# Loading weight tiles early, converting the first two sooner, moving the first up product and scaling chunk 3 sooner: one change to the start of a fused retention and MLP kernel

## The chip, the cores and the metric

The kernel runs on one core of a Trainium2 chip. The metric is device time in microseconds (us). Engines are called as in the profile: PE is TensorE (PEld its weight loads), DVE is VectorE, ACT is ScalarE, POOL is GpSimd, SP the queue that issues the loads.

## The reference, cut to what matters

```python
# retention: B=4, H=8, S=768, D=64, float32
for t in range(S):
    state = gamma * state + k[:, :, t] (outer) v[:, :, t]
    y[:, :, t] = scale * q[:, :, t] @ state
x = y.transpose(0, 2, 1, 3).reshape(3072, 512)
# MLP: w_in 512 x 2048, w_out 2048 x 512
h = x @ w_in
g = h - tanh(h)
out = g @ w_out
```

The two weight matrices arrive in double precision. q, k and v are float32.

## The kernel before

The retention is done in 24 chunks of 128 tokens. A chunk is scaled, k and q are transposed on PE, products give the masked scores and the state, and `outputs` and `outputs_rest` give y, which ScalarE copies to xT. The MLP then takes 256 tokens at a time: an up product `h`, a chain of activations called shrink on ScalarE and VectorE, and a down product `o`. The two are interleaved in one hand-written order. In these traces each engine does its instructions in the order of the program, so an instruction's place in the list of its engine matters as much as its data: raw tile 4 left the load queue at 23.6 us, and ScalarE, busy with other activations, first read it at 43.73.

The weights' 32 raw tiles are converted to float32 on the chip. Each conversion is two steps on ScalarE, four on VectorE, two on GpSimd:

```python
nc.scalar.activation(head.bitcast(F32), hi.bitcast(F32), AF.Abs)
nc.scalar.activation(low, lo, AF.Copy, scale=2.0 ** -52)
nc.vector.tensor_scalar(head..., HI_MIN, HI_MAX, op0=ALU.max, op1=ALU.min)
nc.vector.tensor_scalar(head, head, 3, 0x3FFFFFF8, ...)
nc.vector.scalar_tensor_tensor(head, in0=hi, scalar=0xC0000000, in1=head, ...)
nc.vector.tensor_scalar(power, head, 0xFF800000, None, op0=ALU.bitwise_and)
nc.gpsimd.tensor_tensor(low, low, power.bitcast(F32), op=ALU.mult)
nc.gpsimd.tensor_tensor(dst, low, head, op=ALU.add)
```

Tiles 0 and 1 are what the first up product multiplies by, tiles 2 and 3 the second; tiles 4 and 5 belong to the first down product. The start of the order, which the change touches:

```python
load_chunk(0); load_chunk(1); load_weights(0); load_weights(1); load_chunk(2)
# ... chunks 0 and 1 scaled, transposed; products(0)
outputs(0); products(1); outputs_rest(0)
load_chunk(3); load_weights(2); convert(0); load_weights(3)
outputs(1); convert(1); load_weights(4); outputs_rest(1)
scale_chunk(2, nc.vector); turn(2, "o"); turn_copy(2)
up_step(0)
products(2)
scale_chunk(3, nc.vector); turn(3, "o"); turn_copy(3)
convert(2); load_weights(5); outputs(2); products(3); outputs_rest(2)
load_chunk(4); convert(3); outputs(3); load_chunk(5); load_weights(6)
outputs_rest(3)
shrink_step(0); up_step(1); convert(4); load_weights(7)
shrink_step(1); scale_chunk(4); convert(5); load_weights(8)
up_step(2); turn(4); turn_copy(4); shrink_step(2)
downs(LAG)        # the first down product
# ... (cut)
```

(Statements are joined on lines here.) A raw tile has three buffers, so tile i can be loaded only when tile i-3 has been read (in the trace of this kernel the load queue waited 67.0 and 88.2 us in total for VectorE to have read a raw tile).

## Time and profile before

| | before |
|---|---|
| median, three runs first taken | 791.33 us |
| PE busy, whole span | 759.3 us of 789.4 (96%) |
| PE idle before 85 us | 25.3 us |
| PE waits of that, longest | 5.3 us for tile 5, 4.5 us for the first load of k, 2.8 us with nothing visible that held it ("issue"; called fetch stall below, as it ends at 18.22, 2.7 us after a packet of the page's queue "q8 instruction" begins at 15.54), 1.7 us each for VectorE's scaled q of chunk 2, for that of chunk 3, and for tile 3 |
| PE's mean granted clock, 20 to 60 us | 0.76 |

What is to be won lies in the first tenth of the run, where PE alternates between short attention work and waits. The prediction shows the lines and reads them.

### The profile page before, as it was taken

What the parts mean: (1) busy time and instruction counts of PE and PEld (TensorE: products, weight loads), DVE (VectorE), ACT (ScalarE), POOL (GpSimd) and SP (SyncE); (2) the same over time, 40 slices, a digit from 0 to 9 for tenths busy, and PEclk for the clock granted to TensorE, in tenths of its full rate; (3) what the DMA queues carried; (4) which work ended last, traced back from release to release, by engine and by line L of the source; (5) the groups of instructions that cost most, each with busy time, mean ns of one, the idle gap of its engine ahead of it and who ended that gap; (6) DMA issues with size and microseconds to landing.
All of it is one profiled execution on the core that took longest, in us unless ns stands there. A gap on an engine that the chain in (4) does not pass through costs nothing.

```text
span 789.4 us, 13758 instructions
## 1 busy us (share of the span) xinstructions
PE 759.3 (96%) x5504; PEld 511.7 (65%) x5504; DVE 522.1 (66%) x806; ACT 370.5 (47%) x661; POOL 126.5 (16%) x108
## 2 busy tenths in 40 slices
PE   4769999999999999999999999999999999999997
PEld 3545666667667767666666666666666666666664
DVE  3586598788888865576665565666565666655654
ACT  3363565666565554444444443344444434444432
POOL 1354454433445341000000000000000000000000
PEclk9777999999999999999999999999999999999999
DMA  9465564453343422000000000000000000000000
GB/s 209 123 158 122 122 149 107 119 132 100 95 116 99 94 55 69 29 37 18 1 27 1 0 27 0 1 27 1 1 26 1 27 1 0 27 0 1 27 0 27
DMA packets 85711, 42.97 MB, mean 54 GB/s; under 512 B 76304, under 2 KB 76432, under 8 KB 85648
## 3 DMA queue, kind: packets, MB, share of 16 engines
q1 hardware_dynamic: 85504, 41.95, 21.1%
q8 instruction: 43, 0.70, 0.4%
q10 hardware_dynamic: 144, 0.15, 0.1%
q14 instruction: 20, 0.16, 0.1%
HBM read 35.80 MB, written 6.29 MB: 53 GB/s over the span
## 4 chain that ended last, share of the span: by engine, by line
PE 90%; DVE 6%; issue 1%; POOL 1%; DMA 1%; ACT 1%; SPq 1%; DVEq 0%; ACTq 0%; POOLq 0%
PE h L346 42%; PE o L378 41%; PE y L290 3%; PE kqTp L216 2%; PE s L250 1%; PE s L244 1%; DVE head L169 1%; DVE head L167 1%; DVE a L254 1%; DMA v<-in_v_dram 1%; SPq L192 1%; DVE power L171 0%; DVE g L370 0%; DVE head L165 0%; DVE state L267 0%
## 5 line engine op out<-in xcount | busy, mean ns | idle before, releaser
L378 PE MATMUL o<-w,g 128*128 128x512 f32 x768 | 351.8, 601 | 5.8 <-POOL w L176 5.3
L346 PE MATMUL h<-xT,w 128*128 128x256 f32 x1536 | 354.0, 384 | 1.7 <-POOL w L176 1.7
L346 PEld LDWEIGHTS h<-xT,w 128*128 128x128 f32 x1536 | 292.1, 192 | 70.7 <-issue 30.4
L378 PEld LDWEIGHTS o<-w,g 128*128 128x128 f32 x768 | 145.4, 192 | 152.6 <-issue 138.1
L355 ACT ACTIVATE u<-h 128x512 f32<-128x512 f32 x96 | 57.4, 598 | 267.6 <-PE h L346 267.6
L360 DVE TENSOR_TENSOR th<-h,th 128x512 f32<-128x512 f32 x96 | 66.2, 690 | 158.3 <-ACT th L356 158.2
L370 DVE COPY_PREDICATED g<-large,th 128x512 f32<-128x512 int32 x96 | 74.6, 777 | 9.9
L365 DVE SCALAR_TENSOR_TENSOR h<-q,h 128x512 f32<-128x512 f32 x96 | 66.8, 696 | 11.1 <-DVE h L363 1.4
L363 DVE SCALAR_TENSOR_TENSOR h<-q,h 128x512 f32<-128x512 f32 x96 | 66.9, 696 | 10.4 <-DVE h L361 0.5
L357 ACT ACTIVATE q<-u,tab 128x512 f32<-128x512 f32 x96 | 69.5, 724 | 0.0
L358 ACT ACTIVATE q<-u,tab 128x512 f32<-128x512 f32 x96 | 69.2, 720 | 0.0
L359 ACT ACTIVATE large<-u,tab 128x512 f32<-128x512 f32 x96 | 68.9, 717 | 0.0
L369 DVE TENSOR_TENSOR g<-h,u 128x512 f32<-128x512 f32 x96 | 66.3, 691 | 3.3
L361 DVE SCALAR_TENSOR_TENSOR h<-u,h 128x512 f32<-128x512 f32 x96 | 65.8, 685 | 0.0
L172 POOL TENSOR_TENSOR low<-low,power 128x512 f32<-128x512 f32 x32 | 41.2, 1288 | 151.2 <-DVE power L171 135.2
L356 ACT ACTIVATE th<-h 128x512 f32<-128x512 f32 x96 | 57.0, 594 | 0.0
L226 ACT COPY kqT<-kqTp 128x1024 f32<-128x1024 f32 (+1 forms) x28 | 24.8, 891 | 55.6 <-PE kqTp L216 55.6
L254 DVE TENSOR_TENSOR a<-s,tab 128x512 f32<-128x512 f32 x24 | 16.6, 690 | 43.8 <-PE s L250 43.8
L176 POOL TENSOR_TENSOR w<-low,head 128x512 f32<-128x512 f32 x32 | 41.4, 1293 | 2.5
L324 ACT COPY xT<-y 128x512 f32<-128x512 f32 x24 | 14.1, 587 | 53.3 <-PE y L290 53.3
L169 DVE SCALAR_TENSOR_TENSOR head<-raw,head 128x512 uint32<-128x512 uint32 x32 | 25.5, 797 | 1.1
L201 POOL TENSOR_TENSOR q<-q,tab 128x512 f32<-128x512 f32 x20 | 21.8, 1089 | 22.2 <-DMA q<-in_q_dram 22.2
(32 smaller groups left out, 360.3 us busy)
## 6 DMA issues: line engine op xcount, KB each, us to landing
raw<-in_moe_w_out_dram SPq DMA_DIRECT2D x16, 512.0 KB, 3.7
k<-in_k_dram SPq DMA_DIRECT2D x24, 256.0 KB, 4.6
q<-in_q_dram SPq DMA_DIRECT2D x24, 256.0 KB, 5.1
v<-in_v_dram SPq DMA_DIRECT2D x24, 256.0 KB, 5.4
out_dram<-sum SPq DMA_DIRECT2D x24, 256.0 KB, 2.0
raw<-in_moe_w_in_dram SPq DMA_DIRECT2D x16, 256.0 KB, 3.0
raw<-in_moe_w_in_dram SPq DMA_DIRECT2D x32, 128.0 KB, 3.5
tab<-in_tables_dram ACTq DMA_DIRECT2D x1, 145.5 KB, 2.5
```

The source lines that it names most:

```text
L346: nc.tensor.matmul(hp[:, ts(i, TH)], w1[:, c, ts(2 * m2 + i, P)], xT[n // 2][:, c, ts(n % 2, TH)], start=(i == 0 and c == 0), stop=(c == N ...
L355: nc.scalar.activation(u, hp, AF.Square)
L357: nc.scalar.activation(q0, u, AF.Square, bias=bias0)
L358: nc.scalar.activation(q1, u, AF.Square, bias=bias1, scale=math.sqrt(A))
L359: nc.scalar.activation(large, u, AF.Relu, bias=bias_m)
L360: nc.vector.tensor_tensor(th, hp, th, op=ALU.subtract)
L361: nc.vector.scalar_tensor_tensor(hp, in0=u, scalar=R, in1=hp, op0=ALU.subtract, op1=ALU.mult, reverse0=True)
L363: nc.vector.scalar_tensor_tensor(hp, in0=q0, scalar=C0, in1=hp, op0=ALU.add, op1=ALU.mult)
L365: nc.vector.scalar_tensor_tensor(hp, in0=q1, scalar=A * C1, in1=hp, op0=ALU.add, op1=ALU.mult)
L369: nc.vector.tensor_tensor(flat, hp, u, op=ALU.mult)
L370: nc.vector.copy_predicated(flat, large.bitcast(I32), th)
L378: nc.tensor.matmul(o_p[j], gT[n, m2][:, i, ts(j, P)], w2[:, 2 * m2 + i], start=(first and i == 0), stop=(last and i == 1))
```

## The change

It means to have the first weights converted earlier, and to keep the load queue from waiting for raw buffers. The chunk buffers of x (tag xT) are five, and three of them are not needed until later, so six raw tiles (3 to 8) are put there. Chunk loads and weight loads move forward accordingly. Tile 0 is converted ahead of chunk 0's output, tile 1 ahead of chunk 1's, and tile 1's last two steps go to VectorE. The first up product stands ahead of chunk 2's transposes, and chunk 3 is scaled before chunk 2's products.

```diff
+            if 3 <= i < 9:
+                if i % 2:
+                    room[0] = xp.tile([P, 2, 2 * BANK], U32, tag="xT", name=f"raws_{i}")
+                raw = room[0][:, (i + 1) % 2]
+            else:
+                raw = stage.tile([P, 2 * BANK], U32, tag="raw", name=f"raw_{i}", bufs=3)
...
-    def convert(i):
+    def convert(i, engine=nc.gpsimd):
...
+    convert(0)
     outputs(0)
     products(1)
     outputs_rest(0)
     load_chunk(3)
-    load_weights(2)
-    convert(0)
-    load_weights(3)
+    for i in range(2, 6):
+        load_weights(i)
+    convert(1, nc.vector)
     outputs(1)
-    convert(1)
-    load_weights(4)
     outputs_rest(1)
+    load_chunk(4)
+    load_weights(6)
+    load_weights(7)
+    up_step(0)
     scale_chunk(2, nc.vector)
     turn(2, "o")
     turn_copy(2)
-    up_step(0)
+    scale_chunk(3, nc.vector)
     products(2)
-    scale_chunk(3, nc.vector)
     turn(3, "o")
     turn_copy(3)
     convert(2)
...            (the later loads move forward in the same way)
```

More of the change, by code (lines that the diff above doesn't have):

```diff
@@ L108 @@
     raws = {}
+    room = [None]
     NW = 2 * NM
@@ L131, in load_weights @@
         if w_out.dtype != F32:
-            raw = stage.tile([P, 2 * BANK], U32, tag="raw", name=f"raw_{i}", bufs=3)
+            if 3 <= i < 9:
[4 more added lines that the diff above has]
+                raw = stage.tile([P, 2 * BANK], U32, tag="raw", name=f"raw_{i}", bufs=3)
             raws[i] = raw
@@ L171, in convert @@
         nc.vector.tensor_scalar(power, head, 0xFF800000, None, op0=ALU.bitwise_and)
-        nc.gpsimd.tensor_tensor(low, low, power.bitcast(F32), op=ALU.mult)
+        engine.tensor_tensor(low, low, power.bitcast(F32), op=ALU.mult)
         head = head.bitcast(F32)
@@ L175, in convert @@
             low, head = (t.rearrange("p (k n) -> p k n", k=2) for t in (low, head))
-        nc.gpsimd.tensor_tensor(dst, low, head, op=ALU.add)
+        engine.tensor_tensor(dst, low, head, op=ALU.add)
     loaded = {}
@@ L458 @@
     convert(2)
-    load_weights(5)
     outputs(2)
@@ L462 @@
     outputs_rest(2)
-    load_chunk(4)
+    load_chunk(5)
     convert(3)
     outputs(3)
-    load_chunk(5)
-    load_weights(6)
     outputs_rest(3)
+    load_weights(8)
+    load_chunk(6)
     shrink_step(0)
@@ L471 @@
     convert(4)
-    load_weights(7)
     shrink_step(1)
@@ L475 @@
     convert(5)
-    load_weights(8)
     up_step(2)
@@ L484 @@
     convert(6)
-    load_chunk(6)
     load_weights(9)
```

## The prediction

> **What bounds the kernel now.** I first read the page's busy line by slices: TensorE (PE) is 90% or more in every slice from the eighth on, and low only in the first five (about 99 us); its granted clock is below full only there.
>
> ```profile
> span 789.4 us, 13758 instructions
> PE   4769999999999999999999999999999999999997
> DVE  3586598788888865576665565666565666655654
> PEclk9777999999999999999999999999999999999999
> DMA  9465564453343422000000000000000000000000
> ```
>
> Then busy time by stretches (columns: stretch, length, busy us of PE, PE weight loads, VectorE, ScalarE, GpSimd, each with its count, then PE clock, DMA share, GB/s):
>
> ```profile
> 0.00:20.00 20.00, 9.51 (x256) 7.92 (x256) 7.51 (x14) 6.40 (x13) 2.60 (x6) 0.93 1.09 209
> 20.00:60.00 40.00, 27.48 (x340) 20.87 (x336) 28.30 (x47) 20.51 (x39) 16.44 (x14) 0.76 0.51 142
> 60.00:85.00 25.00, 22.67 (x374) 14.24 (x372) 14.05 (x23) 8.96 (x18) 12.05 (x12) 0.83 0.57 131
> 85.00:130.00 45.00, 44.45 (x640) 32.39 (x641) 38.79 (x60) 28.86 (x53) 20.77 (x17) 1.00 0.57 131
> 130.00:337.00 207.00, 207.00 (x2354) 141.71 (x2353) 160.05 (x265) 115.40 (x212) 74.64 (x62) 1.00 0.35 89
> ```
>
> From 85 us PE is full, and the change leaves PE's list the same length. So the time can only move by PE's idle time before 85 us: 10.49 + 12.52 + 2.33 = 25.3 us, plus what the reduced clock costs there. The rest will only shift.
>
> Third, the chain that ended last, between 14 and 60 us (start, length, what):
>
> ```profile
> 14.74 0.69 PE y L290 x30
> 15.42 2.79 issue
> 18.22 0.83 PE y L290 x14
> ...
> 22.34 0.61 DVE q L201
> 22.95 0.04 issue
> 23.00 1.12 PE kqTp L216 x4
> 24.12 5.30 PE h L346 x16
> 29.42 0.62 PE s L244 x32
> ...
> 32.06 0.61 DVE q L201
> 32.67 0.14 issue
> 32.81 0.64 PE kqTp L216 x4
> ...
> 42.75 1.28 POOL w L176
> 44.03 0.04 issue
> 44.08 4.73 PE h L346 x12
> ...
> 57.92 1.28 POOL w L176
> 59.20 0.04 issue
> 59.24 5.49 PE o L378 x6
> ```
>
> PE is held four times: 2.8 us for nothing visible at 15.4, by VectorE's scaling of chunk 2 (23.00) and of chunk 3 (32.81), by weight tile 3's conversion (44.08), by tile 5's (59.24). The list of waits agrees: matmul h waits 1.7 us and matmul o 5.3 us for GpSimd's last conversion step.
>
> Did any conversion wait for its load? Raw tile 4 left the queue at 23.6 us and 3.4 to 5.3 us is what these tiles take to land, but ScalarE first read it at 43.73, behind five activations. Tile 5 left at about 36.3 and was read at 51.63; tile 7 at about 48.0 and 67.89. No load is late. What is late is each conversion's place in ScalarE's and VectorE's lists.
>
> [...] the clock is 0.50 in 20 to 25 us, and the last 12 matmuls of a 16-matmul product took 4.73 us at 44.08 where a whole one takes 3.45 later. [...] the shift step (line 167) takes 0.43 us, but 1.37 when begun at 38.62 during GpSimd's add (38.32 to 39.71). [...] The trace shows 43 such packets, 0.70 MB[...]: PE stops after about 444 matmul and weight-load instructions and again (0.66 us at 36.6) after about 952, 508 apart[...]. The packets began at 15.5 and 34.3 us.
>
> **The change part by part.**
>
> (a) First up product. Before, chunk 1's output ends on PE at 20.22, but its copy to xT queues behind tile 1's two activations on ScalarE and ends at 21.34; PE does chunk 2's transposes, waits, and starts the product at 24.12. After, tile 1's activations lie before that output, the copy runs at once (0.59 us), and the transposes come later: start at 20.22 + 0.04 + 0.59, about 21.0. Is tile 1 ready? VectorE now converts tile 0 (2.1 us) before chunk 1's mask and states, ending near 17; it then does four steps for tile 1 (2.1 us) and both last steps in GpSimd's place, 2 x 0.69 = 1.4 instead of 2 x 1.29. Even if GpSimd's work on tile 0 blocks it to about 18.0 it ends near 21.5, and the product first needs tile 1 after a quarter of its matmuls. Gain here 3.1 us. The 5.3 us length I leave at about 5.2, mostly at half clock; end 26.2.
>
> (b) The moved transposes. Chunk 2's two groups now stand behind the product: 1.1 us, and products of chunk 2 wait for the second copy (0.59), so their end is 26.2 + 1.1 + 0.1 + 0.6 + 0.75 = 28.75, against 30.50 before: 1.75 left of the 3.1.
>
> (c) Chunk 3 scaled earlier. Before, VectorE scaled it after chunk 2's mask and states; its transposes ended 2.94 us after chunk 2's products. After, that scaling is long done and they take 1.25: 30.0 instead of 33.44. Gain so far 3.4 us.
>
> (d) Tiles 2 and 3. Their order on ScalarE and VectorE after chunk 3's transposes is unchanged. Before, tile 2's VectorE part started at 34.67 and tile 3 was finished at 44.02, 9.35 us later[...]. After, 31.25 + 9.35 = 40.6. Gain 3.4.
>
> (e) Instruction fetch. [...] The early loads make DMA busy there: about 2.35 MB more (tile 5, chunk 4, tiles 6 and 7) at the 0.22 MB/us of the first 28 us fills 28 to 38 us. [...] So the stall may grow from 0.66 to 1.5 or 3 us; chunk 2's last copy and tile 3's activations lie behind it, with some 0.9 us to spare against VectorE's chain. I take off 0.4.
>
> (f) Early raw loads. They remove waits of the DMA queue (raw tiles waited 67 and 88 us in total for VectorE to free a buffer), none of which PE sees. Chunk 7's scaling waited 2.45 us for its load at 80.7, but PE had other work. Zero.
>
> (g) Behind tile 3: second product, its shrink, tile 5, first down product keep order and length. Tile 5 ends near 55.8 instead of 59.2. All that follows shifts.
>
> Sum: 3.1 - 1.35 + 1.65 - 0.4 = 3.0 us[...]. 791.3 - 3.3 = 788.0.
>
> **The rivals.** First, the wait merely changes its name: tile 3's conversion holds the second product whenever the first is done, because convert(2) and convert(3) keep their places. For it: both are released by ScalarE's list, and VectorE's two steps are on the chain from 34.67 to 41.3. Against: that list itself hangs on chunk 3's transposes, which do come sooner. It would leave 0 to 1 us, 790.5 to 791.3. Second, fetch and DMA: under heavier traffic PE's instructions or chunk 3 come 2 to 3 us later. For it: the 2.79 us stall under full load; against: these fetches are few. Result 790 to 791.5, with bad luck 792. Third, loads were the limit after all, and the 5.3 us wait at 59.24 goes too: 783. Against: the 20 us between tile 4's issue and its first use. Fourth, the clock: [...] That is plus or minus 1.5 us.
>
> **Range and chances.** The sum is 3.3 us[...], and one side open by a shorter wait for tile 5: 785.0 to 790.8 should hold it 8 times in 10. Faster by over 2% would need 15.8 us, most of the 25.3 us of early holes: 2 in 100. Slower by 2% would need a new wait in each of the later steps, which the unchanged order forbids: 1 in 100. Within 2%: 97 in 100.
>
> **What would show it.** Right: the first 16-matmul h group starts near 21 and ends near 26; chunk 3's transposes come without a wait for VectorE; the second h product still waits for GpSimd's conversion, ending near 40.6; the first o group still waits 4 to 6 us and resumes near 56; from 85 us on the same rows about 3 us earlier. Wrong: an issue stall over 2 us between 30 and 36; the wait for tile 3 or tile 5 gone; the h group starting after 23; or later stretches with PE under 99%.

The sum came to 3.3 us: 3.0 us from the steps (a) to (e), and 0.3 us for the clock. The clock's term was the author's estimate, not shown by a trace. "Such packets" are those of "q8 instruction". That PE waits for them is the reading of their times: in the kernel before, the stalls end 2.7 and 2.3 us after packets that begin at 15.54 and 34.3.

## The result, and the profile after

Six runs each, taken together: 788.44 us median (786.5 to 789.02) against 791.63 us (789.71 to 793.42) for the kernel before. The ratio is 0.9957, interval 0.9939 to 0.9976: 0.4% faster, inside the 2% that count as the same. Ratios here are the mean time of one kernel's fast runs over that of the other's fast runs of the same rounds, so not quite the ratio of the medians.

The stretches of the changed kernel (columns as in the prediction):

```profile
0.00:20.00 20.00, 9.85 (x240) 7.94 (x240) 10.00 (x18) 6.80 (x12) 2.81 (x6) 0.96 1.09 204
20.00:60.00 40.00, 29.32 (x350) 21.89 (x351) 27.72 (x47) 19.96 (x39) 14.70 (x12) 0.76 0.72 186
60.00:85.00 25.00, 22.26 (x410) 15.26 (x409) 13.76 (x23) 10.97 (x22) 11.69 (x10) 0.88 0.47 105
85.00:130.00 45.00, 45.00 (x610) 31.71 (x609) 39.12 (x62) 29.19 (x54) 21.75 (x18) 1.00 0.50 117
```

VectorE does 10.0 us of work in the first 20 us instead of 7.5, because the conversions have moved there. PE's idle time in 20 to 60 us falls from 12.5 to 10.7 us; over the whole span PE is busy 759.3 and 758.9 us, so most of the gain is idle time. From 85 to 130 us PE is now full, where the kernel before still had 0.55 us of holes. The spans, 789.4 and 786.7 us, differ by 2.7 us, which is already there at 57 us. The chain that ended last shows it (start, length, what):

```profile
16.88 0.46 PE y L297 x14
17.34 1.76 issue
19.10 0.83 PE y L297 x14
...
21.17 0.59 ACT xT L331
21.76 0.14 issue
21.90 5.26 PE h L353 x16
27.16 0.45 PE kqTp L223 x4
...
39.75 1.28 POOL w L183
41.03 0.04 issue
41.07 5.08 PE h L353 x12
...
55.29 1.27 POOL w L183
56.56 0.04 issue
56.61 5.49 PE o L385 x6
```

Against the kernel before, the first h product begins at 21.90 instead of 24.12, tile 3's conversion ends at 41.03 instead of 44.03, and tile 5's at 56.56 instead of 59.20. The two waits behind those conversions remain: PE's idle time for tile 5 is 5.3 us in both, that for tile 3 is 2.24 us instead of 1.70. In this profile the change moves the whole stair, that is, the row of waits one behind the other, by 3.0 us at tile 3 and 2.6 us at tile 5. The two waits of 1.7 us for VectorE's scaled q of chunks 2 and 3 are gone; the fetch stalls and the waits for the two conversions stay.

### The profile page after: what moved, and what is told of

The parts are those of the page before. It is cut to its first block, busy times and chain, and to the rows that moved or that the text cites. A ratio compares the mean times of both kernels' runs of the same rounds, so it can differ in the third digit from the quotient of the medians.

```text
span 786.7 us, 13754 instructions
## 1 busy us (share of the span) xinstructions
PE 758.9 (96%) x5504; PEld 511.9 (65%) x5504; DVE 522.2 (66%) x808; ACT 370.2 (47%) x661; POOL 123.7 (16%) x106
## 4 chain that ended last, share of the span: by engine, by line
PE 92%; DVE 4%; SPq 1%; issue 1%; ACT 1%; POOL 1%; DMA 1%; DVEq 0%; POOLq 0%; ACTq 0%
PE o L385 42%; PE h L353 42%; PE y L297 3%; PE kqTp L223 2%; PE s L257 1%; PE s L251 1%; SPq L199 1%; DVE head L176 1%; DVE head L174 1%; DMA raw<-in_moe_w_in_dram 1%; DVE a L261 0%; DVE power L178 0%; POOL low L179 0%; POOL w L183 0%; DVE head L172 0%
## 5 line engine op out<-in xcount | busy, mean ns | idle before, releaser
L179 POOL TENSOR_TENSOR low<-low,power 128x512 f32<-128x512 f32 x31 | 39.6, 1277 | 157.4 <-DVE power L178 153.7
L183 POOL TENSOR_TENSOR w<-low,head 128x512 f32<-128x512 f32 x31 | 39.8, 1283 | 2.4
L297 PEld LDWEIGHTS y<-kqT,state 64*64 64x64 f32 x704 | 12.9, 134 | 17.9 <-issue 11.7
```

## The experiments

Twelve kernels ran in three batches, each with the kernel before beside it (medians 791.62, 791.78 and 791.64 us). Five runs undo one part of the change each, two keep one part or two, four go further, one repeats the change. The change has a sixth part that no run undoes alone: tile 1's place ahead of chunk 1's output. The changed kernel itself ran only in the first batch and in the rounds of the result, so comparisons with it from the other two batches go across batches; the third batch ran on another chip (recorded as 4, the others as 2), where the kernel before had nearly the same median.

First a warning that these runs taught. Run after run of one kernel differs by up to 5 us (788.9 to 793.9 for the kernel before), largely in step with the granted clock. Of the 31 runs of the kernel before in the three batches, 17 had a mean clock of 0.980 and a median of 792.2 us; the 14 with 0.984 to 0.989 had 789.7 us. The changed kernel (12 runs) shows the same: nine at 0.982 with a median of 788.5 us, three at 0.984 to 0.987 with 786.5 us. Each kernel has one trace (the changed kernel two, both of the low class), so the cause is read across kernels. There the difference is a lower granted clock late in the start. It meets, or does not meet, the same eight matmuls of the second down product, as in the changed kernel (first line, run at 0.982; clock 0.68 over these matmuls, 0.50 from 74 to 76 us) and in one of the experiments (up0_back, second line, run at 0.987; clock 1.00 from 70 to 76 us):

```profile
72.62 5.40 PE L385 MATMUL o<-w,g 128*128 128x512 f32 x8
```

```profile
71.52 4.05 PE L385 MATMUL o<-w,g 128*128 128x512 f32 x8
```

That is 1.35 us with no change to what these instructions wait for. The six matmuls behind the wait for tile 5 give another 0.95 us (5.49 and 4.54 us, at a mean clock of 0.50 and 0.63). Where it matters below, medians are also compared at like clock: the low class up to 0.983, the high class from 0.984. This comparison is rough. The high class of the changed kernel has three runs, the class reaches from 0.984 to 0.991, single runs fall outside the pattern (793.9 us at 0.987), and the mean clock may itself be partly an outcome of the change: the nine runs of tile5_earlier and late_tile5, in which most of PE's 5.3 us wait for tile 5 is gone, were all at 0.984 to 0.986. But so were the five runs of tile1_pool, at 0.984 to 0.987, in which that wait stays.

### after_again: the changed kernel once more

No edit.

> The changed kernel once more, as the yardstick of this batch: about 0.9957 of the kernel before, 788.4 us, with the first h product beginning near 21.9 us, the second held until about 41.0 and the first o group until about 56.6.

788.33 us, ratio 0.9967 (0.9945 to 0.9988). The repeat holds in time, but its profiled execution (789.97 us, the slowest of its six) has a different shape: the first product began at 21.44, and the second fetch stall was long. Here is the same instruction in the first profile and in this one; the bracket is PE's idle time before it, "issue" meaning that nothing visible held it:

```profile
33.45 0.33 PE L297 MATMUL y<-a,v 64*64 64x64 f32 x4 [0.42 <-issue]
```

```profile
35.98 0.33 PE L297 MATMUL y<-a,v 64*64 64x64 f32 x4 [2.48 <-issue]
```

Tile 3 was then waited for until 42.5 and tile 5 until 58.2, against the expected 41.0 and 56.6. So the growth of this stall that the prediction's step (e) feared exists, but not in every execution. Against the kernel before, this profile has only 1.6 us of the gain at tile 3 and 1.1 us at tile 5.

### late_loads: the change without its loads

```diff
-            if 3 <= i < 9:
-                ...                      # room of the x buffers
-            else:
-                raw = stage.tile(..., bufs=3)
+            raw = stage.tile(..., bufs=3)
# and every load_weights and load_chunk back where the kernel before has it
```

> The changed order of conversions, scalings and products, but every raw tile in its three old buffers and loaded where the kernel before loads it. My theory (the loads were never late, the order is what gains): the same as the changed kernel within 0.5 us, about 788.4, PE's waits for tiles 3 and 5 ending near 41 and 56.5. The rival (the early loads gain): back to about 791.5.

787.76 us, ratio 0.996 (0.9941 to 0.9978). No loss at all; at low clock 788.0 against the changed kernel's 788.5. PE waits for tile 3 until 40.44 and for tile 5 until 55.92. The second fetch stall is absent: the waits of PE list one "issue" wait before y, of 1.6 us, instead of two. The waits for tiles 3 and 5 are there as in the changed kernel:

```profile
40.44 8.47 PE L347 MATMUL h<-xT,w 128*128 128x256 f32 x28 [2.19 <-POOL w L177]
55.92 5.49 PE L379 MATMUL o<-w,g 128*128 128x512 f32 x6 [5.27 <-POOL w L177]
```

The rival, that the early loads gain, falls.

### loads_only: the kernel before with the early loads alone

```diff
# the changed kernel, with the compute order of the kernel before:
-    convert(0)
     outputs(0)
...
+    convert(0)
     outputs(1)
+    convert(1)
# and the up product and chunk 3's scaling in their old places
```

> The kernel before with the early loads alone, its order of work untouched. My theory: about 791.6, no gain, tile 3's wait ending near 44 and tile 5's near 59 as before; PE's fetch stalls may grow by some tenths under the heavier traffic. The rival: about 788.4.

792.24 us, ratio 1.002 (0.9998 to 1.0041). The early loads gain nothing here either, and may cost some tenths. Two waits of PE in its trace are longer than in the kernel before (1.74 us for q of chunk 2, 0.66 us of "issue" there):

```profile
24.00 1.11 PE L223 MATMUL kqTp<-tab,q 128*128 128x128 f32 x4 [3.01 <-DVE q L208]
39.48 0.33 PE L297 MATMUL y<-a,v 64*64 64x64 f32 x4 [1.75 <-issue]
```

Tile 3 is waited for until 46.21 and tile 5 until 61.67, not near 44 and 59 as expected. That is one profiled execution; the interval of the times reaches 1. What is shown is that no gain comes from the loads; whether they cost something stays open.

### up0_back: the first up product back behind chunk 2's transposes

```diff
-    up_step(0)
     scale_chunk(2, nc.vector)
     turn(2, "o")
     turn_copy(2)
+    up_step(0)
     scale_chunk(3, nc.vector)
     products(2)
```

> The changed kernel with the first up product back behind chunk 2's transposes and copy. By the changed kernel's times the transposes would end near 23.2, the product near 28.4, and chunk 2's products, whose copies are then long done, near 29.6, where the changed kernel has 29.5. So my theory: no difference within 0.5 us; what counted was that VectorE and ScalarE were ready, not which of the two PE did first. The rival (that order is the gain): 2 to 3 us more.

786.31 us, ratio 0.994 (0.9919 to 0.996): not slower, and by the medians 2 us faster than the changed kernel. At like (high) clock it is 786.3 against 786.5 us, no difference. Five of its six runs are of the high class, three of twelve for the changed kernel. Whether the order itself makes the good clock more frequent, or chance did, these runs can't settle. The trace agrees with the expectation:

```profile
21.87 1.12 PE L223 MATMUL kqTp<-tab,q 128*128 128x128 f32 x4 [0.65 <-DVE q L208]
22.78 5.26 PE L353 MATMUL h<-xT,w 128*128 128x256 f32 x16
```

The transposes still come first, but wait 0.65 us for VectorE's scaled q instead of 1.74, because VectorE has tile 1 behind it earlier. The product begins at 22.78, 1.1 us sooner than in the kernel before (23.91 by the same view), and chunk 2's products need no wait for the copies behind it. Tile 3's wait ends at 40.76, where the changed kernel has 41.07.

### scale3_back: chunk 3's scaling back behind chunk 2's products

```diff
-    scale_chunk(3, nc.vector)
     products(2)
+    scale_chunk(3, nc.vector)
     turn(3, "o")
```

> The changed kernel with chunk 3's scaling back behind chunk 2's products on VectorE. My theory: chunk 3's second transposes wait some 1.5 us for VectorE again and everything behind them moves, 1.5 to 2 us more than the changed kernel, about 790.2. The rival (that wait was hidden behind another): no difference, 788.4.

788.95 us, ratio 0.9976 (0.995 to 1.0002). The old wait is back, at its old length of 1.71 us (the changed kernel has none there):

```profile
31.47 0.85 PE L223 MATMUL kqTp<-tab,q 128*128 128x128 f32 x4 [1.71 <-DVE q L208]
```

Tile 3 is waited for until 43.24 and tile 5 until 59.18, 2.2 and 2.6 us later than in the changed kernel's first profile, but only 0.7 and 1.0 us later than in its second (after_again). The median moves by only 0.6 us, less than expected, with five of its six runs in the high clock class. There it is 788.4 against 786.5 us, 1.9 us more, as expected. The classes are small (five and three runs), so the size is rough; the returned wait is plain.

### tile0_later: tile 0 converted behind chunk 0's output

```diff
-    convert(0)
     outputs(0)
     products(1)
     outputs_rest(0)
+    convert(0)
```

> The changed kernel with tile 0's conversion back behind chunk 0's output. My theory: converting tile 0 first is what made the first h product begin at 21.4 to 21.9 instead of the predicted 21.0, since chunk 1's mask and state now stand behind four VectorE steps; so y of chunk 1 no longer waits for VectorE's state near 16, the h product begins near 21.0, and the time is 0.5 to 1 us less than the changed kernel's. The rival (the fetch stall at 15 to 19 us sets that start whatever VectorE does): no difference.

789.19 us, ratio 0.9965 (0.9944 to 0.9985), and my theory was wrong. VectorE's state is no longer waited for, yet PE stands at the same place for longer, and the product begins at 21.94 as before:

```profile
19.45 0.21 PE L297 MATMUL y<-kqT,state 64*64 64x64 f32 x1 [3.58 <-issue]
21.94 1.62 PE L353 MATMUL h<-xT,w 128*128 128x256 f32 x3 [0.80 <-ACT xT L331]
```

When PE gets there earlier, the stall is longer (3.58 us against 1.76) and ends no sooner (19.45 against 19.10). The fetch stall, not VectorE, sets this start; the rival holds. The time is not better than the changed kernel's: 0.8 us more by the medians, and at high clock 789.5 (five runs) against 786.5 us. Its trace has tiles 3 and 5 waited for until 42.45 and 58.25, close to after_again's 42.50 and 58.16. Whether tile 0's early place gains, these runs don't settle.

### tile1_pool: tile 1's last two steps back on GpSimd

```diff
-    convert(1, nc.vector)
+    convert(1)
```

> The changed kernel with tile 1's last two steps back on GpSimd. My theory: GpSimd would finish tile 1 near 23.1 us, and the first h product (beginning near 21.9, at half clock, its first quarter without tile 1) reaches it near 23.6, so no difference, within 0.5 us of the changed kernel. The rival (VectorE's conversion is what lets the product begin early): 1 to 1.5 us more.

786.69 us, ratio 0.9945 (0.9931 to 0.9959); all five runs of the high clock class, where the changed kernel has 786.5. No difference, as expected: GpSimd finishes tile 1 at 23.15, and the product is at work from 21.05, on its first quarter until then; its fifth matmul begins at 23.20, about 0.3 us late. Taking these steps to VectorE gained nothing that the times show.

### two_parts: only tiles 0 and 1 sooner, and chunk 3 scaled sooner

```diff
# late_loads, and in it:
-    up_step(0)
     scale_chunk(2, nc.vector)
     turn(2, "o")
     turn_copy(2)
+    up_step(0)
     scale_chunk(3, nc.vector)
```

> Only what my theory still counts: tiles 0 and 1 converted sooner and chunk 3 scaled sooner; late loads and the first up product back behind chunk 2's transposes. My theory: all of the gain and a little more, since PE has no second long fetch stall: 785.5 to 787.5, as the run with that product back (786.3). The rival (the loads and the product's place, each without effect alone, cover for each other): 790 or more.

785.81 us, ratio 0.9928 (0.9916 to 0.9941), in the expected range. So the loads and the product's place do not cover for each other: without both, the kernel is at least as fast as with both. At high clock it is 785.8 against 786.5 us; the changed kernel's 788.4 contains mostly runs of low clock. Its trace has the first fetch stall (1.7 us) and not the second.

### tile5_earlier and late_tile5: the wait that the change left

The change leaves PE's longest wait, 5.3 us for tile 5, untouched. Tile 5's conversion stands behind the second shrink on ScalarE and VectorE:

```diff
     up_step(1)
+    scale_chunk(4)
     convert(4)
+    convert(5)
     shrink_step(1)
-    scale_chunk(4)
-    convert(5)
```

> The changed kernel with tile 5's conversion right behind tile 4's, ahead of the shrink of the second product, and chunk 4's scaling ahead of both. My theory (tile 5 is late only by its place in the lists of ScalarE and VectorE, which are idle for some 4 us before that shrink): the 5.3 us wait of the first o group goes, with it the half clock behind it (its last six matmuls in 2.6 us instead of 5.5), so 6 to 8 us less than the changed kernel, about 781.5. The rival (something else holds that group next, a load, the shrink or the scaling of chunk 4): 1 to 3 us less, about 786.

783.75 us, ratio 0.9912 (0.9892 to 0.9932): 4.6 us less than the changed kernel in the same batch, below the expected 6 to 8 and above the rival's 1 to 3. But all five runs are of the high clock class; against the changed kernel's three such runs it is 2.75 us, inside the rival's range. Most of the wait went, and with it the half clock behind it (granted clock 1.00 from 54 to 58 us, where these matmuls had 0.50 in the changed kernel):

```profile
54.10 2.84 PE L385 MATMUL o<-w,g 128*128 128x512 f32 x6 [1.01 <-POOL w L183]
68.34 0.70 PE L297 MATMUL y<-kqT,state 64*64 64x64 f32 x16 [2.62 <-DVE state L270]
```

The first line is the group that began at 56.61 and took 5.49 us. The second shows where part of it was given back: VectorE, now without a hole, has the conversions of tiles 6 and 7 ahead of chunk 5's state, and PE waits 2.62 us for that instead of 0.86. The trace adds up: 4.28 us of the wait and 2.65 us of the six matmuls gained, 1.34 us lost because tile 3's wait ended later (42.41, behind a fetch stall of 2.12 us), 1.76 us lost at that state. That leaves 3.8 us, and the y group behind the second down product begins at 79.11 instead of 82.92. The rival was right that something else holds PE next, but only in part of the size.

> The kernel with the late loads (old three buffers) and tile 5's conversion ahead of the second shrink. My theory: early loads are not needed for it either, and without them the second fetch stall of PE (2.1 us near 34 in the run with the early loads) is short or gone: 1 to 2.5 us less than that run, 781 to 782.5. The rival (tile 5's earlier conversion lives on the early load): ScalarE waits for raw tile 5, 784 to 786.

783.46 us, ratio 0.9897 (0.9875 to 0.9919), with the three old raw buffers. The early load isn't needed for this either. It is hardly faster than the run with the early loads, 783.5 against 783.75 us, so the expected 1 to 2.5 us did not come. Against late_loads, of another batch, with the same buffers, it is 4.3 us less. The second fetch stall is gone, as expected, but PE waits for tile 3 until 41.52 in its profile and again 2.6 us for chunk 5's state.

### tiles_2_3_5 and tiles_2_3_4_5: further in that direction

```diff
# two_parts with tile 5 earlier; convert(3) leaves its later place; and:
     scale_chunk(3, nc.vector)
+    convert(2)
     products(2)
     turn(3, "o")
     turn_copy(3)
-    convert(2)
+    convert(3)
# tiles_2_3_4_5 also:
+    scale_chunk(4)
+    convert(4)
     shrink_step(0)
     up_step(1)
-    scale_chunk(4)
-    convert(4)
```

> On top of those two parts: tile 2 converted ahead of chunk 2's products, tile 3 in tile 2's old place, tile 5 right behind tile 4. My theory (ScalarE and VectorE idle at 22 to 28 us can take tile 2): PE's wait for tile 3 near 37 to 41 goes, and the wait for tile 5 shrinks to about 3 us, since VectorE is then busy to 47 us: about 780.5. The rival (another wait takes its place in full): 783.5, as with tile 5 alone.

784.57 us, ratio 0.9909 (0.9893 to 0.9924), a miss: no better than with tile 5 alone. The wait for tile 3 is gone as expected. In its place came a fetch stall of 2.2 us in front of it and a longer wait for tile 5:

```profile
53.64 4.64 PE L379 MATMUL o<-w,g 128*128 128x512 f32 x5 [2.71 <-POOL w L177]
```

> The same with tile 4 ahead of the first shrink as well. My theory: tile 5 is finished about 1 us sooner, the third h product waits about 1 us for its bank instead: 779 to 780.5. The rival (VectorE's queue is full there, so order no longer matters): the same as the run before it.

782.33 us, ratio 0.9886 (0.987 to 0.9903): the fastest of all, 1.2% under the kernel before and 6 us under the changed one by the medians (4.2 us at high clock). It is slower than the expected 779 to 780.5. The third h product waits for its bank as foreseen (1.94 us for VectorE's last shrink step), and the down group then runs unbroken, at a granted clock of 1.00 (48 to 54 us):

```profile
44.80 3.69 PE L347 MATMUL h<-xT,w 128*128 128x256 f32 x16 [1.94 <-DVE g L370]
49.20 4.00 PE L379 MATMUL o<-w,g 128*128 128x512 f32 x8
```

What was lost is again the 2.62 us for chunk 5's state, at 64.59. With the early waits of PE filled, VectorE's list ahead of that state is the longest wait that PE has left after 50 us; that removing it would gain was not tried.

## Why the prediction was right, and where its steps were not

The predicted 788.0 us met the measured 788.44. The forecast mechanism is what both traces of the changed kernel show: the waits for VectorE's q go, and the waits for tiles 3 and 5 stay and move with what releases them. That the shift comes out at 3 us is in part luck, as the sum below shows. Two readings of the kernel before were slightly off: PE is "held four times", but five holds are listed, and PE is not quite full from 85 us, as 0.55 us of holes are left there. One of the prediction's own signs of being wrong did appear: after_again has an issue stall of over 2 us (2.48) between 30 and 36. Point by point:

- (a) First product, 24.12 to "about 21.0", gain 3.1. Measured 21.90 and 21.44 in two profiles, gain 2.2 and 2.7. What the step missed is that the fetch stall ends later, at 19.10 instead of 18.22. It ends 2.7 us after an instruction packet begins in the kernel before and in this one, and that packet began at 16.39 instead of 15.54. Some 0.4 us of this was there before anything that the change moves: the second transposes of chunk 0 stand at 6.81 instead of 6.45. What delayed the rest is open. A second surprise is that raw tile 0 lands only at about 13.05, and ScalarE waits 0.79 us for it, so PE waits 0.63 us for chunk 1's state; tile0_later shows that this isn't what sets the start, for there PE's wait is gone and the stall ends at 19.45.

```profile
13.10 0.68 ACT L170 ACTIVATE head<-raw 128x512 f32<-128x512 f32 x1 [0.79 <-DMA raw<-in_moe_w_in_dram]
```

  The step also credited the product's place ahead of the transposes. Wrong as a cause: up0_back undoes it and loses nothing. What its trace shows instead is that VectorE is done with tile 1 sooner when q of chunk 2 is to be scaled (PE waits 0.65 us for it, before 1.74); tile 1's earlier place, which should do this, was not undone alone.
- (b) The transposes take part of it back: chunk 2's products were forecast to end at 28.75; they end at 29.50, 1.0 us sooner than before instead of 1.75.
- (c) Chunk 3's transposes end at 30.48, forecast 30.0; 2.96 us sooner instead of 3.4. That their wait of 1.71 us is on the path was right: scale3_back brings the wait back, with 2.2 to 2.6 us behind it by the first profile of the changed kernel and 0.7 to 1.0 us by the second.
- (d) Tile 3 finished at 41.03, forecast 40.6: the same 9.3 us length from tile 2's first VectorE step (31.77), including one step (L174) that took 1.37 us instead of 0.43, begun at 35.62 during GpSimd's add (35.39 to 36.71).
- (e) The fetch stall "may grow to 1.5 or 3 us": 0.42 in one profile, 2.48 in the other, 1.75 with the loads alone, none with late loads. Right as a risk, but only some executions have it; in the first profile the 0.4 us taken off for it was not needed. From chunk 3's second transposes to the start of the next instruction packet it was about 0.7, 3.2 and 2.2 us with the early loads (the changed kernel, after_again, loads_only), and 1.5 and 0.3 us with the old raw buffers (the kernel before, late_loads). What asks for the packet is not shown. That heavier loads delay it fits part of this, but was not isolated: tiles_2_3_5 has a stall of 2.2 us without them.
- (f) Early raw loads worth zero: right, shown by late_loads and loads_only from both sides.
- (g) Tile 5's wait unchanged: right, 5.3 us. Its end, 56.56, is 2.6 us sooner, forecast 3.4. The step that "order and length" stay missed is that the last 12 matmuls of the second product took 5.08 us instead of 4.73, at a mean clock of 0.56 instead of 0.60.

The sum came out because errors cancelled. In the first profile, step (a) gave 0.9 us too little; (b) took 0.1 us less back than forecast, (c) gave 0.3 us more, and the 0.4 us for the fetch were not lost; the second product lost 0.35 us again. That makes 2.6 us where the sum said 3.0, and this trace's span is 2.7 us shorter. The 0.3 us added for the clock is not seen in it; the medians differ by 3.2 us. The second profile has the first product at 21.44, 0.4 us behind the forecast, taking 6.19 us, and a long second stall, and with them only 1.1 us of gain at tile 5. The range of 785.0 to 790.8 held all of the changed kernel's twelve runs (785.5 to 790.0); it needed most of its width, since the runs alone spread over 4.5 us.

The rival "the wait only changes its name" was half right: tile 3's conversion does hold the second product in both kernels, but it moves with what releases it. The rival of fetch and DMA nearly came true in one execution: after_again's profiled run took 789.97 us, with the stall of 2.48 us. The rival of the clock (plus or minus 1.5 us) did too, in both directions: the first product took 5.26 us in one profile (mean clock 0.70) and 6.19 us in the other (0.59). The rival "loads were the limit" fell.

## What to carry to other kernels

A load that no engine on the critical path waits for was not worth a buffer here: before moving loads forward, look whether the first reader waits for the transfer or stands behind other work in its engine's list. Here the place in the list mattered where the loads did not, and the longest wait yielded to moving tile 5's conversion ahead of one shrink (2.7 to 4.6 us), until the next wait was for the engine that does the conversions. Undo the parts of a change one at a time: of the five parts undone here, three (the loads, the first product's place, tile 1's steps on VectorE) could be taken back without loss, one brought a wait of PE back (chunk 3's scaling), and one is open (tile 0's place).
